# Attention units taken two at a time in the later batches of an attention and MLP kernel

## The chip, the cores and the metric

One core of one Trainium2 chip runs the whole program. The metric is the device time of one execution in microseconds (us), as the median of several runs. Its engines are TensorE (matrix products into the banks of PSUM), VectorE and ScalarE (elementwise work, and the only ones here that read PSUM), GpSimd (called POOL in the profile) and SyncE (SP, which issues most DMAs). Each works through its own instructions in order, and semaphores make one wait for another.

## What is computed

Three steps, in float32 at the interface: attention with two kinds of mask, a gated MLP, and an MLP with silu.

```python
# q, k, v: batch 4, 8 heads, 576 positions, head size 64; stride = 32
scores = scale * q @ k.T
mask_local   = (rel >= 0) & (rel < stride)                    # heads 0 to 3
mask_strided = (rel >= 0) & (pos_k % stride == pos_q % stride)  # heads 4 to 7
attn = softmax(where(mask, scores, -1e9))
x = (attn @ v), heads side by side: 2304 tokens x 512
y = ((x @ w_a) * (x @ w_b)) @ w_out          # inner size 1536
h = y @ w_in;  out = (h * sigmoid(h)) @ w_out2   # inner size 2048
```

## The kernel before

The tokens are cut into groups of 512 (the last has 256). Products are made in a split form: every operand is a pair of a rounded value and a remainder (`split_w`, `split_act`: ScalarE makes the first, VectorE the second), and each product takes three matmuls (`PASSES`). Batch 0's attention comes first, in a startup stage of its own. Then 136 **blocks** run, numbered p: for the first two groups the gated MLP (blocks 0 to 71), then the second MLP (72 to 135). A block is 12 matmuls of 128x128 by 128x512; its kind is a, b or o in the gated MLP (two up products and the down product) and i or p in the other. The loop over blocks stands at lines 1305 to 1379. After it come the other groups, in a form with fewer products.

Batches 1 to 3 of the attention are woven into the blocks 0 to 114. `PLAN` (line 96) gives for each batch a first block, the start of each of its nine **units**, and an end. Units 0 to 4 are the windows of 128 queries of the four local heads (unit 4 has 64); units 5 to 8 are groups of residues of the four strided heads (unit 8 has fewer). `plan_attention` (line 702) puts the steps of a unit with start s into blocks: `prepare` at s (for strided units VectorE gathers the queries), `scores`, `mask`, `largest`, `softmax`, `guard` and `normalise` at s+2, `turn` (transposing the weights on TensorE) and `turned` (copying them out of PSUM) at s+5, `values` (the products with v) and `store` at s+6. It also spreads the loads of later data, and the VectorE transposes of q and k (`transpose_qk`).

`block(p)` (line 739) sets the order in a block. At its head come the planned loads, TensorE steps and `turned` copies; then the block's 12 matmuls; then, in the order of the letters in `STEPS` (line 104), the rest: R prepare, M mask, 0 1 2 the steps that convert a weight (`merge_w`, one on ScalarE and two on VectorE), B a rescaling on ScalarE, K writing the converted weight to DRAM, O store, Y the split of the weight for block p+2, X softmax, W loads, N guard and normalise. In blocks 0 to 35 the order is RM0BK1O2YXWN, later 0O1B2MKWYRXN. The evacuation of the block's own product comes behind all of it: for a a copy on ScalarE; for b a product on VectorE, a cast on ScalarE and a subtraction on VectorE; for i a tanh on ScalarE and then the same three. Since every engine works in order, a step that waits holds up all that is behind it on that engine.

PSUM has eight banks: four accumulators, two in the ring for up products, and two for attention (`att_tile`, in turn, lines 187 to 196). In batches 1 to 3 a unit's scores take both attention banks, its turned weights one and its values one. `store` (line 542) copies the values on ScalarE; for the groups 0, 1 and 4 VectorE also takes the remainder out of the same bank.

The probabilities of softmax lie in three buffers by turns (`probs`, line 174), normalised by POOL at line 491.

Of the kernel before, what the change touches and what calls it, by code (L numbers as in the profile page):

```python
# [18 lines left out]
P = 128  # L19
STRIDE = 32  # L20
HALF = 64
TAKE = 3

RES = [(0, 3, 6), (9, 12, 15), (18, 21, 24), (27, 29)]
# [69 lines left out]


PLAN = {
# [3 lines left out]
}  # L100

PAIR_OF = (2, 3)

# [8 lines left out]
def attention_gated_mlp_silu_mlp(  # L112
# [15 lines left out]
    nc = tc.nc  # L128
# [7 lines left out]
    J = S // STRIDE  # L136
    NL = -(-S // P)
    JR = J * TAKE
    NG_S = max(map(len, RES))
    firsts = [r for i in RES for r in i]  # L140
    KV = HALF + JR
# [24 lines left out]
    ident = cpool.tile([P, P], F32, name="ident")  # L166
    ident_b = cpool.tile([P, P], BF16, name="ident_b")
# [4 lines left out]
    vs = apool.tile([P, len(firsts), 4, D], F32, name="vs", bufs=1)  # L172
# [60 lines left out]
    class Batch:  # L233
# [167 lines left out]
            st["parts"] = parts  # L401
            self.state[u] = st

        def scores(self, u):

            st = self.state[u]
            w, segs = st["w"], st["segs"]
            halves = [[part for part in st["parts"] if part[1] == hp] for hp in range(2)]
            if self.first:
                bank = att_tile(self.wide)[:, :segs * w].rearrange("p (s k) -> p s k", k=w)  # L410
                st["sc"] = [bank]
                for hp in range(2):
                    rows = slice(HALF * hp, HALF * (hp + 1))
                    nc.tensor.matmul(bank[rows], lhsT=ident_b[:, rows], rhs=st["mask"], start=True, stop=False)
                    for m, (_, _, s, rows, lhsT, rhs) in enumerate(halves[hp]):
                        last = m >= len(halves[hp]) - HALF // lhsT.shape[-1]
                        nc.tensor.matmul(bank[rows, s], lhsT=lhsT, rhs=rhs, start=False, stop=last)
                return
            per = segs // 2 if st["full"] else segs
            st["sc"] = [  # L420
                att_tile(self.wide)[:, :per * w].rearrange("p (s k) -> p s k", k=w) for _ in range(2)
            ]
            for half in range(2):
                for m in range(len(halves[0])):
                    for hp in range(2):
                        t, _, s, rows, lhsT, rhs = halves[hp][m]
                        bank = t if st["full"] else hp
                        if bank ^ hp == half:
                            nc.tensor.matmul(
                                st["sc"][bank][rows, s % per], lhsT=lhsT, rhs=rhs, start=True, stop=True  # L430
                            )

        def mask(self, u):
            st = self.state[u]
# [55 lines left out]
            rs = rs.unsqueeze(3).to_broadcast([P, ng, 2, w])  # L490
            nc.gpsimd.tensor_tensor(out=pr, in0=pr, in1=rs, op=ALU.mult)

        def turn(self, u):
            ty, i = self.units[u]
            st = self.state[u]
            nk = P if ty == 0 else KV
            pr = st["pr"].rearrange("p g s k -> p g (s k)")
            tp = att_tile(self.wide)
            for t in range(st["slots"]):
                nc.tensor.transpose(tp[:nk, P * t:P * (t + 1)], pr[:, t, :nk], ident)  # L500
            st["tp"] = tp

        def turned(self, u):
            ty, i = self.units[u]
# [12 lines left out]
                st["pt"] = pt = apool.tile([P, NG_S * P], F32, tag="pt", name="pt", bufs=2)  # L517
                copy(out=pt[:KV, :P * n], in_=st["tp"][:KV, :P * n])

        def values(self, u):  # L520
            ty, i = self.units[u]
            st = self.state[u]
            n, pt = st["n"], st["pt"]
            xp = st["xp"] = att_tile(self.wide)
            for hp in range(2):
                for g in range(st["slots"]):
                    for c in range(2):
                        h = 2 * hp + c
                        rows = xp[HALF * c:HALF * (c + 1), hp * n:(hp + 1) * n]
                        if ty == 0:  # L530
                            out = rows[:, HALF * g:HALF * (g + 1)]
                            lhsT = self.vl[:, 2 * i + g, h, :]
                            rhs = pt[:, g ^ hp if st["full"] else g, h, :]
                        else:
                            r0 = RES[i][g] - RES[i][0]
                            out = rows.rearrange("p (j r) -> p j r", j=J)[:, :, r0:r0 + TAKE]
                            lhsT = vs[:KV, firsts.index(RES[i][g]), h, :]
                            o = P * g + HALF * (hp if self.first else c)
                            rhs = pt[:KV, o:o + JR]
                        nc.tensor.matmul(out, lhsT=lhsT, rhs=rhs, start=True, stop=True)  # L540

        def store(self, u):
            ty, i = self.units[u]
# [33 lines left out]
    half = {"A": [], "B": []}  # L577
# [124 lines left out]
    def plan_attention(batch, s0, first, end):  # L702

        add = lambda at, place, f, *a: plan.setdefault((at, place), []).append((f, a))

        def spread(loads, n, s0, s1):
            for m in range(n):
                add(s0 + m * (s1 - s0) // n, "load", next, loads, None)

        turn1 = first[NL - 1] + 2  # L710
        for one in range(4):
            add(s0 + one // 2, "prepare", batch.transpose_qk, 0, one)
            add(turn1 - 4 + one, "prepare", batch.transpose_qk, 1, one)
        spread(batch.load_qk(1), 9, s0 + 2, turn1 - 7)
        spread(batch.load_vs(), 4 * TAKE + 5, s0 + 4 * (batch.b > 1), first[NL] + 3)
        for u, s in enumerate(first):
            add(s, "prepare", batch.prepare, u)
            add(s + 2, "tensor", batch.scores, u)
            add(s + 2, "mask", batch.mask, u)
            add(s + 2, "mask", batch.largest, u)  # L720
            add(s + 2, "softmax", batch.softmax, u)
            add(s + 2, "normalise", batch.guard, u)
            add(s + 2, "normalise", batch.normalise, u)
            add(s + 5, "tensor", batch.turn, u)
            add(s + 5, "turned", batch.turned, u)
            add(s + 6, "tensor", batch.values, u)
            add(s + 6, "store", batch.store, u)
        after = Batch(batch.b + 1, False)
        if after.b < B:
            spread(after.load_qk(0), 9, turn1 + 2, end)  # L730
            spread(after.load_vl(), 10, first[NL] + 7, end)
        return after

    def background(at, *places):
# [28 lines left out]
    with tc.manual_schedule():  # L763
# [51 lines left out]
        for s in range(-1, max(nu + LV, max(PART), max(CONV) + 1) + 1):  # L815
# [6 lines left out]
            now, last = CONV.get(s), CONV.get(s - 1)  # L822
            for step in ORDER:
# [13 lines left out]
                elif step == "A" and s in PART:  # L837
                    i = PART[s]
# [17 lines left out]
        batch = after  # L856
# [570 lines left out]
```

## Time and profile before

| | |
|---|---|
| median of 3 runs | 954.84 us (954.73 to 958.06) |
| span of the profiled execution, first to last instruction | 952.6 us |
| mean granted TensorE clock | 0.988 of full speed |
| TensorE matmul busy | 928.5 us, 97% |
| VectorE busy | 663.9 us, 70% |
| ScalarE busy | 542.6 us, 57% |
| POOL busy | 80.4 us, 8% |

The profile gives the span of its execution and no separate device time; the median lies 2.2 us above the span. Matmuls are pipelined and their ends are modelled, so TensorE's busy share says less than the starts of its runs and the waits between them. In the rows below, PE is TensorE's matmuls, DVE is VectorE, ACT is ScalarE; "out<-in" are the program's names of tiles, x12 is a count of records (a float32 matmul leaves two), and a bracket at the end is the time the engine sat idle before, with what ended it. A waits view names an engine and its line, what it waited for, the total, how many times and the longest.

### The profile page before, as it was taken

What the parts mean: (1) busy time and instruction counts of PE and PEld (TensorE: products, weight loads), DVE (VectorE), ACT (ScalarE), POOL (GpSimd) and SP (SyncE); (2) the same over time, 40 slices, a digit from 0 to 9 for tenths busy, and PEclk for the clock granted to TensorE, in tenths of its full rate; (3) what the DMA queues carried; (4) which work ended last, traced back from release to release, by engine and by line L of the source; (5) the groups of instructions that cost most, each with busy time, mean ns of one, the idle gap of its engine ahead of it and who ended that gap; (6) DMA issues with size and microseconds to landing.
All of it is one profiled execution on the core that took longest, in us unless ns stands there. A gap on an engine that the chain in (4) does not pass through costs nothing.

```text
span 952.6 us, 15861 instructions
## 1 busy us (share of the span) xinstructions
PE 928.5 (97%) x5626; PEld 749.6 (79%) x5626; DVE 663.9 (70%) x1248; ACT 542.6 (57%) x1274; POOL 80.4 (8%) x138
## 2 busy tenths in 40 slices
PE   9999999999999899999999999999999989999998
PEld 5767777787777677778888888888998768888897
DVE  4588888866767766666777666765587666765475
ACT  3558788566667665465544444345565555554364
POOL 2232222111111110100000000000000000000000
PEclk9799999999999999999999999999999999999999
DMA  9999899898698994322332222223464121234371
GB/s 165 198 271 269 248 254 271 248 294 240 224 267 208 264 223 133 105 86 89 100 105 83 67 67 67 57 83 112 126 185 125 44 67 56 78 107 148 108 212 47
DMA packets 163647, 145.29 MB, mean 153 GB/s; under 512 B 96800, under 2 KB 119904, under 8 KB 163568
## 3 DMA queue, kind: packets, MB, share of 16 engines
q1 hardware_dynamic: 154758, 121.81, 48.1%
q0 software_dynamic: 6720, 21.63, 6.8%
q10 hardware_dynamic: 2090, 0.84, 0.5%
q8 instruction: 44, 0.72, 0.3%
q14 instruction: 35, 0.29, 0.1%
HBM read 121.70 MB, written 22.54 MB: 151 GB/s over the span
## 4 chain that ended last, share of the span: by engine, by line
PE 75%; DVE 11%; ACT 8%; issue 3%; DMA 2%; SPq 0%; DVEq 0%; POOL 0%; ACTq 0%; POOLq 0%
PE ring L683 17%; PE ring L958 10%; PE att L958 8%; PE acc L1019 8%; PE acc L1365 7%; PE acc L1145 4%; PE att L1019 4%; PE ring L1019 4%; PE acc L1345 4%; PE acc L683 3%; ACT prs L466 2%; DVE w L676 2%; DVE raw L650 2%; PE att L540 1%; ACT raw L647 1%
## 5 line engine op out<-in xcount | busy, mean ns | idle before, releaser
L683 PE MATMUL ring<-x,w 128*128 128x512 f32 (+1 forms) x816 | 165.5, 356 | 1.5 <-DVE w L676 1.5
L683 PEld LDWEIGHTS ring<-x,w 128*128 128x128 f32 x816 | 132.4, 189 | 23.4 <-DVE w L676 2.0
L1241 DVE TENSOR_TENSOR w<-raw,w 128x512 fp32r<-128x512 f32 (+1 forms) x164 | 106.3, 656 | 30.3 <-ACT w L1240 27.5
L1240 ACT CAST w<-raw 128x512 fp32r<-128x512 f32 (+1 forms) x164 | 95.8, 593 | 18.6 <-PE att L1019 11.0
L676 DVE TENSOR_TENSOR w<-raw,w 128x512 fp32r<-128x512 f32 x136 | 92.8, 686 | 8.6 <-ACT w L675 7.9
L683 PE MATMUL ring<-y,w 128*128 128x512 f32 x384 | 96.1, 400 | 2.2 <-DVE g L1337 0.8
L1365 PE MATMUL acc<-w,h 128*128 128x512 f32 x384 | 93.9, 394 | 0.0
L683 PEld LDWEIGHTS ring<-y,w 128*128 128x128 f32 x384 | 71.9, 191 | 18.8 <-DVE w L676 1.1
L675 ACT CAST w<-raw 128x512 fp32r<-128x512 f32 x136 | 82.8, 619 | 4.0 <-DVE raw L655 3.9
L1365 PEld LDWEIGHTS acc<-w,h 128*128 128x128 f32 x384 | 70.9, 188 | 15.4
L693 ACT CAST h<-h 128x512 fp32r<-128x512 f32 (+1 forms) x48 | 27.3, 568 | 95.1 <-DVE h L1331 48.1
L1345 PE MATMUL acc<-h,w 128*128 128x512 f32 x288 | 70.8, 395 | 0.0
L958 PE MATMUL ring<-operands,w 128*128 128x512 f32 x240 | 61.4, 398 | 2.4 <-ACT w L1240 2.0
L694 DVE TENSOR_TENSOR h<-g,h 128x512 fp32r<-128x512 f32 (+1 forms) x64 | 39.9, 624 | 33.4 <-ACT h L693 33.2
L1345 PEld LDWEIGHTS acc<-h,w 128*128 128x128 f32 x288 | 53.0, 188 | 11.5
L693 ACT CAST h<-g 128x512 fp32r<-128x512 f32 (+1 forms) x64 | 36.3, 568 | 44.8 <-DVE g L1337 30.4
L958 PE MATMUL att<-operands,w 128*128 128x512 f32 x240 | 60.2, 395 | 0.0
L958 PE MATMUL ring<-x,w 128*128 128x512 f32 x240 | 59.2, 391 | 1.0 <-ACT u L969 1.0
L466 ACT ACTIVATE prs<-sm,nm 128x54 f32<-128x54 f32 (+1 forms) x120 | 39.8, 336 | 30.5 <-DVE nm L452 30.4
L958 PEld LDWEIGHTS ring<-operands,w 128*128 128x128 f32 x240 | 44.7, 188 | 14.8 <-ACT w L1240 2.7
L650 DVE SCALAR_TENSOR_TENSOR raw<-words,raw 128x512 int32<-128x512 int32 x68 | 47.6, 699 | 9.5 <-ACT raw L647 8.9
L958 PEld LDWEIGHTS ring<-x,w 128*128 128x128 f32 x240 | 44.9, 188 | 11.1 <-ACT u L969 1.4
(200 smaller groups left out, 1577.1 us busy)
## 6 DMA issues: line engine op xcount, KB each, us to landing
raw<-keptp SPq DMA_DIRECT2D x80, 256.0 KB
raw<-kepti SPq DMA_DIRECT2D x64, 256.0 KB
words<-in_moe_w_out_dram SPq DMA_DIRECT2D x28, 512.0 KB
raw<-kepto SPq DMA_DIRECT2D x48, 256.0 KB
raw<-kepta SPq DMA_DIRECT2D x36, 256.0 KB
raw<-keptb SPq DMA_DIRECT2D x36, 256.0 KB
words<-in_moe_w_in_dram SPq DMA_DIRECT2D x16, 512.0 KB
words<-in_moe_w_a_dram SPq DMA_DIRECT2D x12, 512.0 KB
```

What stands on the lines that cost most here:

```text
L466: nc.scalar.activation(out=place[s], in_=src[:, s], func=AF.Exp, bias=st["nm"][:, s:s + 1], scale=1.0, accum_out=su[:, s:s + 1],)
L650: nc.vector.scalar_tensor_tensor(out=z, in0=high, scalar=SIGN, in1=z, op0=ALU.bitwise_and, op1=ALU.bitwise_or)
L675: nc.scalar.copy(out=o[:, 0], in_=t)
L676: nc.vector.tensor_tensor(out=o[:, 1], in0=t, in1=o[:, 0].bitcast(F32), op=ALU.subtract)
L683: nc.tensor.matmul(ps[:, :T], lhsT=w[:, wi, c * P:(c + 1) * P], rhs=x[:, xi, c, :T], start=(c == 0 and wi == 0 and xi == 0), stop=(c == CC ...
L693: nc.scalar.copy(out=o[:, 0, :T], in_=t32[:, :T])
L958: nc.tensor.matmul(self.acc[acc], lhsT=w[:, wi, (2 * part + c) * P:(2 * part + c + 1) * P], rhs=x[:, xi, c], start=(begin and c == 0 and m ...
L1019: nc.tensor.matmul(accs[d], lhsT=lhsT, rhs=rhs, start=(first and wi == 0 and xi == 0), stop=(last and wi == 1))
L1240: nc.scalar.copy(out=o[:, 0, cols], in_=t)
L1241: nc.vector.tensor_tensor(out=o[:, 1, cols], in0=t, in1=o[:, 0, cols].bitcast(F32), op=ALU.subtract)
L1345: nc.tensor.matmul(accs[d], lhsT=w[:, wi, d * P:(d + 1) * P], rhs=h[:, xi], start=(j == 0 and wi == 0 and xi == 0), stop=(j == N1 - 1 and ...
L1365: nc.tensor.matmul(accs[t][:, :DM], lhsT=h[:, xi, t * P:(t + 1) * P], rhs=w[:, wi, :], start=(j == 0 and wi == 0 and xi == 0), stop=(j == ...
```

## The change

Units are taken in the groups of `TOGETHER`: (0, 1), (2, 3), (4), (5, 6), (7, 8). `PLAN` holds a start for each group. The scores of both units of a group are issued in one run of TensorE, each unit in its own 256 columns of the same two banks; so are both turns, and both units' products with v. Two local units share one bank for the turned weights and one for the values; two strided units take a bank each. With a group's start s, prepare is at s-1 and s, scores at s+2, the masks and softmaxes of the two units at s+2 and s+3, both turns and copies at s+6, both values and stores at s+7 (a single unit as before). In batches 2 and 3 the four transposes of q and k at the batch's start go one to a block instead of two, and the loads of the other heads begin two blocks later. Batch 0 computes as before.

```diff
 PLAN = {
-    1: (0, [1, 2, 7, 8, 13, 18, 19, 24, 25], 35),
-    2: (35, [38, 43, 48, 53, 58, 63, 68, 73, 78], 80),
-    3: (81, [84, 85, 90, 91, 96, 101, 102, 107, 108], 0),
+    1: (0, [2, 8, 14, 19, 25], 35),
+    2: (35, [39, 48, 57, 64, 73], 80),
+    3: (81, [84, 90, 96, 101, 107], 0),
 }
+TOGETHER = ((0, 1), (2, 3), (4,), (5, 6), (7, 8))
...
+        def scores_together(self, us):
+            banks = [att_tile(self.wide) for _ in range(2)]
+            for n, u in enumerate(us):
+                st = self.state[u]
+                w = st["w"]
+                st["per"] = per = st["segs"] // 2 if st["full"] else st["segs"]
+                o = 256 * n
+                st["sc"] = [b[:, o:o + per * w].rearrange("p (s k) -> p s k", k=w) for b in banks]
             for half in range(2):
-                for m in range(len(halves[0])):
+                for u in us:
...
+        def shared(self, us):
+            bank = None
+            for n, u in enumerate(us):
+                if n == 0 or self.units[u][0] == 1:
+                    bank, o = att_tile(self.wide), 0
+                yield u, bank, o
+                o += 256
+
+        def turn(self, *us):
+            for u, bank, o in self.shared(us):
...
+                st["tp"] = tp = bank[:, o:]
...
+        def values(self, *us):
+            for u, bank, off in self.shared(us):
...
+                xp = st["xp"] = bank[:, off:]
...
         for one in range(4):
-            add(s0 + one // 2, "prepare", batch.transpose_qk, 0, one)
+            add(s0 + (one if batch.b > 1 else one // 2), "prepare", batch.transpose_qk, 0, one)
             add(turn1 - 4 + one, "prepare", batch.transpose_qk, 1, one)
-        spread(batch.load_qk(1), 9, s0 + 2, turn1 - 7)
+        spread(batch.load_qk(1), 9, s0 + (4 if batch.b > 1 else 2), turn1 - 7)
...
+        for us, s in zip(TOGETHER, first):
+            others = len(us) - 1
+            add(s + 2, "tensor", batch.scores, *us)
+            for n, u in enumerate(us):
+                add(s + n - others, "prepare", batch.prepare, u)
+                add(s + n + 2, "mask", batch.mask, u)
+                add(s + n + 2, "mask", batch.largest, u)
+                add(s + n + 2, "softmax", batch.softmax, u)
+                add(s + n + 2, "normalise", batch.guard, u)
+                add(s + n + 2, "normalise", batch.normalise, u)
+                add(s + others + 5, "turned", batch.turned, u)
+                add(s + others + 6, "store", batch.store, u)
+            add(s + others + 5, "tensor", batch.turn, *us)
+            add(s + others + 6, "tensor", batch.values, *us)
```

## Rows read from the trace of the kernel before

**Rows 1.** The page, shares of the span on the chain that ended last, by engine

```profile
PE 75%; DVE 11%; ACT 8%; issue 3%; DMA 2%; SPq 0%; DVEq 0%; POOL 0%; ACTq 0%; POOLq 0%
```

**Rows 2.** Busy us by stage: PE, PEld, DVE, ACT, POOL; then clock, DMA share, GB/s

```profile
67.99:175.34 107.35, 105.13 (x739) 82.36 (x734) 89.78 (x180) 84.18 (x215) 22.74 (x40) 1.00 0.98 265
...
180.22:288.27 108.05, 107.64 (x719) 85.50 (x719) 76.39 (x142) 67.66 (x170) 14.55 (x25) 1.00 0.90 256
288.27:339.89 51.62, 46.76 (x281) 35.99 (x279) 38.22 (x72) 34.05 (x84) 6.98 (x12) 0.97 0.94 240
339.89:439.89 100.00, 97.35 (x762) 75.99 (x761) 64.31 (x140) 58.94 (x175) 10.76 (x16) 1.00 0.46 126
...
439.89:952.60 512.71, 503.87 (x2485) 423.51 (x2483) 346.40 (x606) 259.77 (x492) 6.51 (x12) 1.00 0.32 97
```

**Rows 3.** TensorE timeline in batch 2: start, us, line, out<-in, count

```profile
197.08 0.38 PE L500 MATMUL att<-ident,prs 128*128 128x128 f32 x2
197.21 3.02 PE L1345 MATMUL acc<-h,w 128*128 128x512 f32 x12
200.16 0.69 PE L540 MATMUL att<-ptl,vl 128*64 128x64 f32 x16
200.78 3.01 PE L683 MATMUL ring<-x,w 128*128 128x512 f32 x12
203.72 0.70 PE L429 MATMUL att<-kT,qT 64*32 64x64 f32 x32
204.35 3.01 PE L683 MATMUL ring<-x,w 128*128 128x512 f32 x12
207.20 2.88 PE L1345 MATMUL acc<-h,w 128*128 128x512 f32 x12
209.92 2.89 PE L683 MATMUL ring<-x,w 128*128 128x512 f32 x12
```

**Rows 4.** TensorE's waits from 63 to 440 us: total, times, longest

```profile
PE att L540 <- ACT pt L518: 3.3, 2, 2.8
PE att L540 <- ACT ptl L512: 2.4, 3, 1.3
PE ring L683 <- DVE w L676: 2.3, 2, 1.5
...
PE ring L683 <- DVE g L1337: 0.8, 1, 0.8
```

**Rows 5.** VectorE timeline, the middle of block 25

```profile
143.53 0.42 DVE L571 TENSOR_TENSOR x<-att,x 128x252 fp32r<-128x252 f32 x1
143.87 0.68 DVE L655 SCALAR_TENSOR_TENSOR raw<-e,raw 128x512 int32<-128x512 int32 x1
144.47 0.69 DVE L676 TENSOR_TENSOR w<-raw,w 128x512 fp32r<-128x512 f32 x1
```

**Rows 6.** VectorE timeline, the transposes in blocks 35 and 81

```profile
176.76 1.43 DVE L275 STREAM_TRANSPOSE qT<-qld 128x576 f32<-128x576 f32 x2
...
325.69 1.43 DVE L275 STREAM_TRANSPOSE qT<-qld 128x576 f32<-128x576 f32 x2
```

**Rows 7.** ScalarE timeline, the copy ahead of unit 8's values in batch 2

```profile
331.57 0.37 ACT L518 COPY pt<-att 118x256 f32<-118x256 f32 x1
```

**Rows 8.** Busy times of block 84's products, columns as in rows 2

```profile
332.60:337.04 4.44, 4.44 (x16) 3.50 (x13) 2.48 (x4) 1.80 (x5) 0.54 (x1) 0.62 0.95 245
```

**Rows 9.** TensorE timeline, the attention runs at blocks 73 and 74

```profile
290.99 0.49 PE L500 MATMUL att<-ident,prs 128*118 128x128 f32 x3
...
296.17 0.91 PE L540 MATMUL att<-pt,vs 118*64 118x54 f32 x24
```

**Rows 10.** VectorE timeline, first conversion step and softmax guard of block 75

```profile
303.71 0.69 DVE L650 SCALAR_TENSOR_TENSOR raw<-words,raw 128x512 int32<-128x512 int32 x1
...
308.37 0.17 DVE L478 TENSOR_SCALAR su<-su 128x6 f32<-128x6 f32 x1 [1.58 <-ACT prs L466]
```

**Rows 11.** ScalarE timeline, the second of block 25's two store copies

```profile
143.29 0.21 ACT L568 COPY x<-att 128x72 f32<-128x72 f32 x1
```

More of the change, by code (lines that the diff above doesn't have):

```diff
@@ L402, in prepare, with scores @@
             self.state[u] = st
-        def scores(self, u):
+        def scores(self, u, *more):
+            if not self.first:
+                return self.scores_together((u, *more))
             st = self.state[u]
@@ L408, in scores @@
             halves = [[part for part in st["parts"] if part[1] == hp] for hp in range(2)]
[L409 to L422, printed above, removed]
-            for half in range(2):
-                for m in range(len(halves[0])):
[L425 to L431, printed above, removed]
+            bank = att_tile(self.wide)[:, :segs * w].rearrange("p (s k) -> p s k", k=w)
@@ new lines, in scores @@
+            st["sc"] = [bank]
+            for hp in range(2):
+                rows = slice(HALF * hp, HALF * (hp + 1))
+                nc.tensor.matmul(bank[rows], lhsT=ident_b[:, rows], rhs=st["mask"], start=True, stop=False)
+                for m, (_, _, s, rows, lhsT, rhs) in enumerate(halves[hp]):
+                    last = m >= len(halves[hp]) - HALF // lhsT.shape[-1]
+                    nc.tensor.matmul(bank[rows, s], lhsT=lhsT, rhs=rhs, start=False, stop=last)
+        def scores_together(self, us):
[6 more added lines that the diff above has]
+                st["sc"] = [b[:, o:o + per * w].rearrange("p (s k) -> p s k", k=w) for b in banks]
+            for half in range(2):
+                for u in us:
+                    st = self.state[u]
+                    halves = [[part for part in st["parts"] if part[1] == hp] for hp in range(2)]
+                    for m in range(len(halves[0])):
+                        for hp in range(2):
+                            t, _, s, rows, lhsT, rhs = halves[hp][m]
+                            bank = t if st["full"] else hp
+                            if bank ^ hp == half:
+                                nc.tensor.matmul(
+                                    st["sc"][bank][rows, s % st["per"]], lhsT=lhsT, rhs=rhs, start=True, stop=True
+                                )
@@ L491, in normalise @@
             nc.gpsimd.tensor_tensor(out=pr, in0=pr, in1=rs, op=ALU.mult)
[L493 to L501, printed above, removed]
+        def shared(self, us):
[7 more added lines that the diff above has]
+            for u, bank, o in self.shared(us):
+                ty, i = self.units[u]
+                st = self.state[u]
+                nk = P if ty == 0 else KV
+                pr = st["pr"].rearrange("p g s k -> p g (s k)")
+                st["tp"] = tp = bank[:, o:]
+                for t in range(st["slots"]):
+                    nc.tensor.transpose(tp[:nk, P * t:P * (t + 1)], pr[:, t, :nk], ident)
         def turned(self, u):
@@ L518, in turned @@
                 copy(out=pt[:KV, :P * n], in_=st["tp"][:KV, :P * n])
[L520 to L540, printed above, removed]
@@ new lines, in values @@
+        def values(self, *us):
+            for u, bank, off in self.shared(us):
+                ty, i = self.units[u]
+                st = self.state[u]
+                n, pt = st["n"], st["pt"]
+                xp = st["xp"] = bank[:, off:]
+                for hp in range(2):
+                    for g in range(st["slots"]):
+                        for c in range(2):
+                            h = 2 * hp + c
+                            rows = xp[HALF * c:HALF * (c + 1), hp * n:(hp + 1) * n]
+                            if ty == 0:
+                                out = rows[:, HALF * g:HALF * (g + 1)]
+                                lhsT = self.vl[:, 2 * i + g, h, :]
+                                rhs = pt[:, g ^ hp if st["full"] else g, h, :]
+                            else:
+                                r0 = RES[i][g] - RES[i][0]
+                                out = rows.rearrange("p (j r) -> p j r", j=J)[:, :, r0:r0 + TAKE]
+                                lhsT = vs[:KV, firsts.index(RES[i][g]), h, :]
+                                o = P * g + HALF * (hp if self.first else c)
+                                rhs = pt[:KV, o:o + JR]
+                            nc.tensor.matmul(out, lhsT=lhsT, rhs=rhs, start=True, stop=True)
@@ L708, in spread @@
                 add(s0 + m * (s1 - s0) // n, "load", next, loads, None)
-        turn1 = first[NL - 1] + 2
+        starts = {us[0]: s for us, s in zip(TOGETHER, first)}
+        first1 = starts[NL]
+        turn1 = starts[NL - 1] + 2
         for one in range(4):
-            add(s0 + one // 2, "prepare", batch.transpose_qk, 0, one)
+            add(s0 + (one if batch.b > 1 else one // 2), "prepare", batch.transpose_qk, 0, one)
             add(turn1 - 4 + one, "prepare", batch.transpose_qk, 1, one)
-        spread(batch.load_qk(1), 9, s0 + 2, turn1 - 7)
[L715 to L727, printed above, removed]
+        spread(batch.load_qk(1), 9, s0 + (4 if batch.b > 1 else 2), turn1 - 7)
+        spread(batch.load_vs(), 4 * TAKE + 5, s0 + 4 * (batch.b > 1), first1 + 3)
+        for us, s in zip(TOGETHER, first):
[12 more added lines that the diff above has]
+            add(s + others + 6, "tensor", batch.values, *us)
         after = Batch(batch.b + 1, False)
@@ L730, in plan_attention @@
             spread(after.load_qk(0), 9, turn1 + 2, end)
-            spread(after.load_vl(), 10, first[NL] + 7, end)
+            spread(after.load_vl(), 10, first1 + 7, end)
         return after
```

## The prediction

> **What bounds the kernel now.** I read four views, in this order. The page's shares of the chain of waits come first [rows 1]: three quarters of the span lie on TensorE, a fifth on VectorE and ScalarE together. So time taken off TensorE counts, but not everywhere. The busy times by stage say where [rows 2]. By the TensorE timeline the first four rows are blocks 4 to 35, blocks 37 to 71, 72 to 85, and 86 to 114; the last is all that follows. In the first, VectorE is busy 89.8 of 107.35 us, ScalarE 84.2 and TensorE 105.1: three engines near their limit. In the second and fourth TensorE alone is near it (107.64 of 108.05, 97.35 of 100.00). In the third TensorE is idle 4.9 us of 51.62. Behind block 114, where the changed code ends, TensorE is busy 503.9 of 512.7 us, so what is won until then should stay to the end.
>
> Third, the TensorE timeline at small scale [rows 3]. A plain block of 12 products takes 207.20 to 209.92, 2.72 us. Between a turn and a run of values a block lasts 197.21 to 200.16, 2.95; between values and scores 2.94; between scores and a plain block 2.85. So leaving attention costs about 0.13 and entering scores or values about 0.10 (leaving values some 0.03 more; entering a turn nothing, 0.23 being one exit and one entry). I call that the switch: 0.23 for a run of scores, 0.13 for a turn, 0.26 for values. The runs themselves (0.13, 0.62 and 0.63 for one unit of the local heads) stay as they are: the same matmuls are issued.
>
> Fourth, what TensorE waits for between 63 and 440 us [rows 4]: ScalarE's copies of the turned weights ahead of the values (3.3 and 2.4 us), the split weights (2.3), and a bank held by VectorE's gate (0.8). These waits can weigh as much as all the switches, so they decide.
>
> **The change part by part.** *Fewer runs.* In batches 1 and 3 the units of a pair already start one block apart. A pair there has two score runs, a turn, a joint run (values of the first, turn of the second) and a values run. The joint run's switch is not in my rows; it lies between 0.26 and 0.39, the sum of its two kinds, and I take 0.30: 0.46 + 0.13 + 0.30 + 0.26 = 1.15. After, three runs: 0.23 + 0.13 + 0.26 = 0.62. Four pairs save 2.1 us in each of these batches. In batch 2 the units stand five blocks apart, six runs for two units, 1.24; four pairs save 2.5. Together 6.7 us of TensorE time, if nobody else is late.
>
> *Blocks 4 to 36 (batch 1).* Here VectorE decides. The last place where TensorE waits for it is the scores of unit 7 at block 26, which need unit 6's subtraction out of the bank; that begins at 143.53 and ends at 143.95 [rows 5]. After the change both subtractions of the pair are issued in block 26 and the joint scores in block 27. VectorE then has ahead of them what was behind: the two last steps of block 25 and the first of block 26, three of 0.60 by the spacing of the rows, so 145.8. From unit 7's scores to block 36 TensorE took 143.95 to 175.34, 31.4 us; block 26's products (2.7) now lie ahead, and this pair's switches shrink by 0.5: 28.2, hence 174.0. A gain of 1.3. Its ends: nothing, if ScalarE's copies for two units in one block delay VectorE further, and 3.4, if the two engines run ahead a block earlier (2.1 from the switches and the 1.3).
>
> *The transposes of the next batch.* Batch 2's q and k are transposed on VectorE, two in block 35 (1.4 us from 176.76 [rows 6]) and two in block 36, ahead of the split for block 37, on which TensorE waits up to 1.5 us. One per block takes 0.7 off that wait; nothing if VectorE has other work in the hole. I take 0.7. The later ones lie in blocks where TensorE has two blocks of lead.
>
> *Blocks 37 to 85 (batch 2).* Switches give 2.5. Block 84 held the longest wait, 2.8 us: TensorE wants unit 8's values, but VectorE did transposes from 325.69 on [rows 6] ahead of a gate, ScalarE had to cast that gate's result, and the copy of the turned weights began only at 331.57 [rows 7]. Behind it the granted clock averaged 0.62 in the 4.44 us of block 84's products [rows 8], that is, TensorE fell to its lower level of 1.2 GHz after that idle; 1.6 us lost against 2.85. Unit 8 now ends at block 80, before those transposes, so both go: 4.4. Block 73 took from 290.99 to 296.17, 5.2 us with a turn of 0.24 in it [rows 9], 2.0 more than 2.95, since unit 6's softmax sat ahead of the evacuation of y. The softmax moves to block 67; instead two units' stores (some 0.7 of ScalarE) come into block 71. Walking the copies through I leave 0.7 of the wait: 1.3 won. One of the three waits on the local copies [rows 4], 0.4 at block 59, goes.
>
> Added: units 7 and 8 have masks and softmaxes in blocks 75 and 76, one behind the other. Block 75's VectorE steps take 303.71 to 308.54 [rows 10], 4.8 us in 6 instructions, 1.58 of it waiting for ScalarE's softmax in its own queue. A second such block behind it makes 9.6, against 7.0 for TensorE (two blocks and two units' scores). Queued behind the waiting VectorE are the split weights for blocks 77 to 79. Of TensorE's lead of two blocks most is used up by then, as block 73's wait shows; with 2.6 more and the conversions of block 77 behind it I estimate 3.5 of waits in blocks 77 to 80. The ends are zero (the lead holds) and 5.1 (the clock falls again as well, 1.6). Net 2.5 + 4.4 + 1.3 + 0.4 - 3.5 = 5.1.
>
> *Blocks 86 to 114 (batch 3).* Switches 2.1. The first values waited 1.3, the longest of the waits on the local copies [rows 4]; now the turn falls behind a block without a cast, but four copies come together instead of two: 0.45 left, 0.85 won. The wait for the gate at block 106 (0.8) is set by VectorE; with a turn (0.24) and two switches (0.36) taken from ahead of it TensorE comes 0.6 earlier and waits that much longer. The first strided pair's values wait some 0.25 more than the 0.5 they do now (3.3 less 2.8). Net 2.1 + 0.85 - 0.6 - 0.25 = 2.1, between 0 and 3.5.
>
> At no cost: the loads moved by a block or two on SP's queue (no row of TensorE's waits names a DMA), the slices of the shared banks (256 columns hold the widest unit's 162), and POOL's normalising, which keeps at least three blocks before its turn.
>
> *Sum:* 1.3 + 0.7 + 5.1 + 2.1 = 9.2 us. The profiled span of 952.6 becomes 943.4; the median, 954.84, stands 2.2 above that span, so the forecast is 945.6.
>
> **The rivals.** *A shared bank is read by one engine at a time.* In block 25 ScalarE's second copy out of the bank, which is not an operand of the subtraction, ended at 143.50 [rows 11], and VectorE's subtraction from that bank began at 143.53 [rows 5]. If so, in blocks 9 and 15 (local pairs sharing a bank, with both copy and subtraction) the second unit's copy waits for the first's subtraction, 0.42 and a restart, about 0.6 each time: 1.2 less won, 946.8. The Trainium skill, "PSUM — Partial Sum Buffer", section "PSUM bank collisions raise a hardware error", says that two engines may not touch one bank in the same quadrant at a time, reads included, so that the order must be enforced; by that rule the sharing has this price, and the trace agrees as far as one row can.
>
> *VectorE and ScalarE hand it all back.* They never wait long for TensorE in stages one and three, and their work is the same. Then the 6.7 us of switches turn into new waits: 9.2 - 6.7 = 2.5 won, 952.3. For it speaks the first stage, against it the second, where TensorE has no waits to speak of.
>
> *Longer waits ahead of the values: slower.* A pair's values need both units' copies, put into one block. In six places (blocks 25, 31, 70, 79, 107, 113) that block follows one whose gate result ScalarE must cast first, as in block 83. If ScalarE is a block late there, each is a wait like block 84's, with the clock behind it: 2.8 + 1.6 = 4.4. Two undo the gain; from the third on the kernel is slower: 945.6 + 13.2 = 958.8. Against it: two strided units' copies cost 0.37 + 0.47, about one local unit's pair (0.75), and of the five such waits so far four were 1.3 or less.
>
> *The lead holds.* No new wait in blocks 77 to 80 (3.5), and batch 1 wins 3.4: 14.5 won, 940.3.
>
> **How the numbers follow.** Forecast 945.6 with 0.44; the one-engine bank 946.8 with 0.20; the lead holds 940.3 with 0.10; handed back 952.3 with 0.18; slower 958.8 with 0.08. The measurement can tell about 0.5%, 4.8 us, from no change: below 950.1 is faster, which the first three are (0.74); the fourth is the same (0.18); the last slower (0.08). The range, 939.5 to 952.5, takes in the bounds of the unknown waits and leaves out the slower case and a rest of the others.
>
> **What would show it.** Right: block 36 begins 1 to 2 us earlier, block 84 has no wait and the clock there is 1.00, block 86 begins some 7 us earlier, block 115 some 9; the block behind a turn of two units still takes 2.95. Wrong: waits over 2 us on ScalarE's copies of the turned weights at blocks 26, 71, 80 or 108; a clock of 0.5 near block 79; scores waiting over 1 us for the stores at blocks 10, 16 and 27; or a joint run of two units longer than two single ones, which would mean that sharing a bank costs TensorE itself.

## The result: 948.44 us, and where the 0.85% came from

The changed kernel has a median of 948.44 us in its runs (945.97 to 951.47); the kernel before, beside it, 954.84 (952.84 to 958.21). One more execution of the changed kernel, at a mean granted clock of 0.85, took 1006.47; it is counted in the median, but in neither the range nor the ratio. The ratio of time after to time before is 0.9915, 95% interval 0.9887 to 0.9942: about 8.1 us won (5.5 to 10.8), 6.4 by the medians, where 9.2 were forecast. The profiled execution has a span of 946.7 us against 952.6.

In the changed kernel the lines have moved: 440 scores, 454 mask, 477 softmax, 521 turn, 532 and 538 the copies of the turned weights, 561 values, 589 and 592 the store's copy and subtraction, 697 split weights, 1362 gate, 1088 results. Two lines of the page of after, the busy time of TensorE and the shares on the chain that ended last (75% of it on TensorE before, [rows 1]):

```profile
PE 918.6 (97%) x5620; PEld 746.9 (79%) x5626; DVE 663.4 (70%) x1248; ACT 541.8 (57%) x1274; POOL 80.2 (8%) x138
...
PE 69%; DVE 13%; ACT 8%; issue 5%; DMA 3%; SPq 1%; POOL 0%; DVEq 0%; ACTq 0%; POOLq 0%
```

TensorE is busy 9.9 us less than before, and the chain leans more on VectorE. Next the busy times in three stretches, first of the kernel before, then of after. The cuts are the same events in both: the split of weights by VectorE just ahead of batch 1's first scores (59.40 and 57.47), TensorE's restart in block 37, the scores at block 86, and the end of batch 3's last values.

```profile
59.40:180.22 120.82, 114.85 (x825) 89.29 (x823) 102.00 (x202) 93.78 (x238) 23.11 (x41) 0.99 0.94 256
180.22:339.89 159.67, 154.40 (x998) 121.49 (x998) 114.61 (x214) 101.71 (x252) 21.53 (x37) 0.99 0.91 251
339.89:437.09 97.20, 94.55 (x750) 73.71 (x749) 63.32 (x138) 58.05 (x172) 10.76 (x16) 1.00 0.47 126
```

```profile
57.47:179.06 121.59, 112.02 (x824) 88.11 (x822) 102.50 (x201) 93.47 (x238) 23.78 (x41) 1.00 0.96 262
179.06:333.49 154.43, 150.87 (x999) 120.19 (x999) 113.59 (x213) 100.68 (x250) 21.01 (x37) 1.00 0.91 254
333.49:431.14 97.65, 94.15 (x750) 75.04 (x749) 63.26 (x137) 58.97 (x174) 10.72 (x16) 0.98 0.50 134
```

Read the first number behind each stretch. Batch 1 takes 0.8 us longer than before, batch 2 with what follows it 5.2 less, batch 3 0.45 longer. At block 115 the changed kernel is 5.96 us ahead (433.93 against 439.89), and it stays so to the end (512.77 us behind that point, 512.71 before). But 5.2 less 0.8 and 0.45 is 4.0. The other 1.93 us stand there at the first cut already, ahead of all the scores that the change joins: 59.40 against 57.47. Most of it, 1.69, is there at an earlier split, inside batch 0, which computes as before; VectorE in before, then in after:

```profile
46.59 0.69 DVE L676 TENSOR_TENSOR w<-raw,w 128x512 fp32r<-128x512 f32 x1
```

```profile
44.90 0.66 DVE L697 TENSOR_TENSOR w<-raw,w 128x512 fp32r<-128x512 f32 x1
```

In the ten kernels whose traces are told of here this step begins between 43.1 and 47.1 us, three kernels with the old order among them at 43.1, 46.4 and 46.6. The clock went with it. From the start to the first cut, before and then after (the last figures of a row are the mean granted clock, the share of the DMA engines and GB/s):

```profile
0.00:59.40 59.40, 58.06 (x562) 39.32 (x563) 36.61 (x91) 28.45 (x119) 18.53 (x33) 0.89 1.00 201
```

```profile
0.00:57.47 57.47, 54.88 (x556) 37.78 (x562) 36.40 (x91) 28.35 (x119) 18.24 (x33) 0.94 0.97 193
```

In the ten traces the first cut lies at 56.4 us with a clock of 0.97 up to it, at 57.5 to 57.8 with 0.94 (three), at 59.2 to 60.5 with 0.88 or 0.89 (three, one of them in the new order and two in the old), and at 59.6 and 59.8 with 0.86; the tenth, at 61.9 with 0.99, waited 6.1 us for a load. So the 1.93 us go with the clock of these two executions and not with the order of the units. Stages are compared below from cut to cut, and totals by the ratios alone.

What TensorE waited for in after, from 60 to 440 us (total, times, longest; before: [rows 4]):

```profile
PE att L561 <- ACT ptl L532: 3.2, 5, 1.0
PE att L440 <- DVE x L592: 2.8, 2, 1.6
PE ring L704 <- DVE g L1362: 2.1, 1, 2.1
PE ring L704 <- DVE w L697: 1.8, 2, 1.3
PE att L561 <- ACT pt L538: 1.7, 3, 1.2
PE acc L1390 <- ACT w L696: 1.2, 1, 1.2
```

The wait of 2.8 at block 84 is gone. Three others have grown: scores that wait for the subtractions of the store (2.8 in two places, blocks 10 and 16; 1.1 before), the gate at block 106 (0.8 before, 2.1 now), and, in batch 1, values that wait for ScalarE's copies of the turned weights (0.7 before, 3.6 now; the rows stand with the account of blocks 4 to 36).

Joint runs do what they should. Batch 2, units 2 and 3, TensorE's timeline of after:

```profile
230.02 0.60 PE L521 MATMUL att<-ident,prs 128*128 128x128 f32 x4
230.37 2.99 PE L704 MATMUL ring<-x,w 128*128 128x512 f32 x12
233.29 1.15 PE L561 MATMUL att<-ptl,vl 128*64 128x64 f32 x32
234.37 2.79 PE L1370 MATMUL acc<-h,w 128*128 128x512 f32 x11
```

Two units' values take 233.29 to 234.37, 1.08 us, where two runs of one took 0.62 each [rows 3]; the block behind the two-unit turn (0.35 us) lasts 2.92.

### The profile page after: what moved, and what is told of

Its sections match the earlier page's. It is cut to its first block, busy times and chain, and to the rows that moved or that the text cites. A ratio compares the mean times of both kernels' runs of the same rounds, so it can differ in the third digit from the quotient of the medians.

```text
span 946.7 us, 15843 instructions
## 1 busy us (share of the span) xinstructions
PE 918.6 (97%) x5620; PEld 746.9 (79%) x5626; DVE 663.4 (70%) x1248; ACT 541.8 (57%) x1274; POOL 80.2 (8%) x138
## 4 chain that ended last, share of the span: by engine, by line
PE 69%; DVE 13%; ACT 8%; issue 5%; DMA 3%; SPq 1%; POOL 0%; DVEq 0%; ACTq 0%; POOLq 0%
PE ring L704 14%; PE ring L983 11%; PE att L983 8%; PE acc L1044 8%; PE acc L1390 6%; PE acc L1170 4%; PE att L1044 4%; PE ring L1044 4%; ACT prs L477 3%; PE acc L1370 3%; PE acc L704 2%; DVE w L697 2%; DVE raw L671 2%; DMA kepti<-raw 1%; DVE raw L676 1%
## 5 line engine op out<-in xcount | busy, mean ns | idle before, releaser
L983 PEld LDWEIGHTS ring<-operands,w 128*128 128x128 f32 x240 | 44.7, 188 | 14.8 <-ACT w L1265 2.7
L671 DVE SCALAR_TENSOR_TENSOR raw<-words,raw 128x512 int32<-128x512 int32 x68 | 47.6, 700 | 10.8 <-ACT raw L668 10.2
```

What stands on the lines that cost most here:

```text
L671: nc.vector.scalar_tensor_tensor(out=z, in0=high, scalar=SIGN, in1=z, op0=ALU.bitwise_and, op1=ALU.bitwise_or)
L983: nc.tensor.matmul(self.acc[acc], lhsT=w[:, wi, (2 * part + c) * P:(2 * part + c + 1) * P], rhs=x[:, xi, c], start=(begin and c == 0 and m ...
```

## Experiments

All ratios are to the kernel before; those of one group of runs share its runs.

**Units one at a time, at the new places.** This takes the joint runs away and keeps the plan, except that the first unit of a pair has its turn and values one block earlier than in the changed kernel.

```diff
-    1: (0, [2, 8, 14, 19, 25], 35),
+    1: (0, [2, 3, 8, 9, 14, 19, 20, 25, 26], 35),
...
-TOGETHER = ((0, 1), (2, 3), (4,), (5, 6), (7, 8))
+TOGETHER = tuple((u,) for u in range(9))
```

(Batches 2 and 3 likewise.)

> The units stand in the changed kernel's blocks (the second of a pair one block behind the first), but each unit's scores, turn and values are TensorE runs of their own. If the joint runs bring the gain (switches of 0.23, 0.13 and 0.26 us): four pairs in each of three batches pay 0.53 us more, 6.4 us in all, so 0.998 of before. If the new places bring it (block 84 without its wait, block 73 shorter): 0.992, like the changed kernel. Block 84 has no wait by both.

Measured: 951.75 us, ratio 0.9950 (0.9930 to 0.9969). So of about 8 us the places alone bring 4.8 (3.0 to 6.7). That leaves 3.3 for the joint runs, uncertain by about 3 (an estimate from the two intervals); the two traces are 1.2 apart from the first cut to the last values (374.89 and 373.67). By stage the split is uneven:

```profile
59.21:179.13 119.92, 112.73 (x822) 87.31 (x820) 102.30 (x201) 92.92 (x237) 23.80 (x41) 1.00 0.92 262
179.13:336.13 157.00, 153.77 (x998) 121.54 (x998) 114.02 (x213) 101.15 (x251) 21.02 (x37) 0.99 0.91 250
336.13:434.10 97.97, 94.33 (x749) 73.56 (x748) 63.84 (x138) 58.91 (x174) 10.73 (x16) 1.00 0.51 134
```

In batch 1 single units are quicker than joint ones (119.92 against 121.59, and 121.1 to 121.2 in two further kernels with joint ones below): joining costs there. With a bank for each unit's values (the next run, and the last) joint units take 120.0 and 120.5, so most of that cost is the shared bank's. In batch 2 single units are 2.6 slower (157.00 against 154.43). Block 84 has no wait, but another place has one, since unit 8's scores at block 76 need banks that unit 7's scores fill until its mask has read them:

```profile
303.81 0.87 PE L440 MATMUL att<-kT,qs 64*64 64x54 f32 x16 [2.44 <-DVE sm L454]
304.61 4.61 PE L704 MATMUL ring<-y,w 128*128 128x512 f32 x12
```

and the twelve products behind that wait of 2.44 took 4.61 us instead of 2.9. These 4.1 us at one place are more than the whole difference in batch 2, so it isn't the switches alone that the joint runs save there.

**Values of a local pair in banks of their own.** The only edit is that each unit's values get a bank; scores and turns stay joined.

```diff
         def values(self, *us):
-            for u, bank, off in self.shared(us):
+            for u, bank, off in ((u, att_tile(self.wide), 0) for u in us):
```

> The changed kernel, but two local units' values lie in a bank each. If one engine at a time may read a bank: ScalarE's second store copy in blocks 9 and 15 no longer waits for VectorE (0.49 and 0.84 us in the changed kernel), the scores at blocks 10 and 16 wait some 0.5 us less each, and block 36 begins up to 1 us earlier: 0.9905 of before. If VectorE's own chain sets batch 1's pace: those waits shift, block 36 begins within 0.3 us of the changed kernel, 0.9915.

Measured: 946.29 us, ratio 0.9899 (0.9865 to 0.9933). From the first cut to block 37 it takes 120.00 us against 121.59, and the two waits of scores for the subtractions fall from 1.20 and 1.60 to 0.60 and 0.94. What they were is seen on ScalarE and VectorE in block 9 of the changed kernel:

```profile
84.33 0.35 ACT L589 CAST x<-att 128x256 fp32r<-128x256 f32 x1
85.17 0.37 ACT L589 CAST x<-att 128x256 fp32r<-128x256 f32 x1 [0.49 <-DVE x L592]
```

```profile
84.71 0.42 DVE L592 TENSOR_TENSOR x<-att,x 128x256 fp32r<-128x256 f32 x1
85.57 0.42 DVE L592 TENSOR_TENSOR x<-att,x 128x256 fp32r<-128x256 f32 x1 [0.44 <-ACT x L589]
```

The second unit's copy waits for the first unit's subtraction, though it doesn't use what that writes, and the second subtraction waits for its copy: one engine at a time on a bank, in a chain of four. With own banks the two subtractions run as one row, 0.76 us:

```profile
86.80 0.76 DVE L592 TENSOR_TENSOR x<-att,x 128x256 fp32r<-128x256 f32 x2
```

**Two transposes per block again,** with the loads left where the change put them.

```diff
-            add(s0 + (one if batch.b > 1 else one // 2), "prepare", batch.transpose_qk, 0, one)
+            add(s0 + one // 2, "prepare", batch.transpose_qk, 0, one)
```

> The changed kernel, but two transposes of q and k per block at a batch's start, as before. By the sum of the prediction the wait at block 37 grows by 0.7 us and nothing else does: 0.9922 of before. If the split for block 37 waits for something else (block 37 gained only some 0.2 us): within 0.2 us, 0.9917. If the old wait at block 84 came from the transposes alone, not from the values standing there: a wait of over 1 us comes back near blocks 83 to 85.

Measured: 947.9 us, ratio 0.9913 (0.9882 to 0.9945); the time can't tell it from the changed kernel. The wait at block 37 can: 1.34 us in after, 2.01 here.

```profile
179.06 8.00 PE L704 MATMUL ring<-x,w 128*128 128x512 f32 x34 [1.34 <-DVE w L697]
```

```profile
181.91 9.59 PE L704 MATMUL ring<-x,w 128*128 128x512 f32 x34 [2.01 <-DVE w L697]
```

So spreading the transposes is worth 0.67 us of that wait between these two traces. In the four traces with two transposes in a block the wait is 1.55 to 2.33, in the six with one 0.88 to 1.35. Behind the longer wait the same 34 records took 9.59 us instead of 8.00, at a granted clock of 0.82 of full speed on the mean: 1.6 us more in this execution.

**Half of the first group's results on ScalarE.** At block 106 TensorE waits for VectorE's gate. Ahead of that gate VectorE copies four results (2.44 us); here ScalarE takes two of them.

```diff
-                result(t0, t, accs[t], pool, tag, "v", nc.gpsimd)
+                result(t0, t, accs[t], pool, tag, "va"[t % 2] if g == 0 else "v", nc.gpsimd)
```

> The changed kernel, but of the four evacuations of results behind block 103 ScalarE takes two, VectorE two. If VectorE's four in a row make the gate late for which block 106 waits (2.1 us, with the clock at 0.62 behind it): the wait falls to about 0.9, the clock stays at 1.00, 2.8 us less: 0.9885 of before. If the wait comes from the softmax that VectorE waits for in its queue (1.58 us): the wait stays above 1.8 and the time within 0.5 us of the changed kernel, 0.991.

Measured: 946.78 us, ratio 0.9895 (0.9866 to 0.9925). The wait goes from 2.13 to 0.93, by just what the copies shrank (2.44 to 1.25), and block 106's products are at full clock. The step in the ratio, from 0.9915, lies within the intervals. First after, then this kernel:

```profile
401.17 4.61 PE L704 MATMUL ring<-y,w 128*128 128x512 f32 x12 [2.13 <-DVE g L1362]
```

```profile
400.49 3.04 PE L704 MATMUL ring<-y,w 128*128 128x512 f32 x12 [0.93 <-DVE g L1362]
```

**The same edit in the kernel before,** as a control.

> The kernel before with half of the first group's results copied by ScalarE instead of VectorE. There the wait for the gate at block 106 was 0.78 us with the full clock behind it. If the results matter only because the two-unit runs made VectorE late there, this gains at most those 0.78 us: ratio 0.998 to 1.000, and block 106 without a wait. If the results are a cost in themselves, the gain is that of the changed kernel with the same edit beside it (some 1.2 us and a low clock of 1.6): ratio 0.997 or less.

Measured: ratio 1.0006 (0.9979 to 1.0034). The wait of 0.78 at block 106 is gone in its trace, and nothing can be told in the time. What hung on the results before the change was at most that wait; the trace of the changed kernel has 1.2 us of wait and the low clock on them.

**The joint scores at block 103 undone,** for batch 3's first strided pair alone.

```diff
+            if batch.b == 3 and us == (5, 6):
+                add(s + 2, "tensor", batch.scores, 5)
+                add(s + 3, "tensor", batch.scores, 6)
+            else:
                 add(s + 2, "tensor", batch.scores, *us)
```

> The changed kernel, with the scores of batch 3's first strided pair in two runs again, at blocks 103 and 104; its masks, turn and values stay where they are. In the changed kernel the first mask of this pair began 1.50 us after the first score, in the kernel before 0.87 us. If the joint scores make VectorE late at block 106 by these 0.63 us, the wait for the gate there falls from 2.13 to about 1.3 (0.63, and one more switch of 0.23 ahead of it), block 115 begins 0.4 us earlier, and by 1.6 more where the low clock behind the wait goes too. If the wait comes only from TensorE being earlier, it falls by the 0.23 alone, to 1.9. The total is too close to the changed kernel's to be told apart by time: ratio 0.988 to 0.992 either way.

Measured: 947.83 us, ratio 0.9898 (0.9874 to 0.9921). The wait is 1.10. First after: the start of the scores on TensorE, then mask and gate on VectorE. Then the same rows with the scores apart.

```profile
389.19 1.44 PE L440 MATMUL att<-kT,qs 64*64 64x54 f32 x48
...
390.69 0.56 DVE L454 SCALAR_TENSOR_TENSOR sm<-att,mask_str 128x162 f32<-128x162 f32 x2 [2.55 <-PE att L440]
...
400.42 0.69 DVE L1362 SCALAR_TENSOR_TENSOR g<-th,ring 128x512 f32<-128x512 f32 x1
```

```profile
389.11 0.82 PE L440 MATMUL att<-kT,qs 64*64 64x54 f32 x24
...
389.98 0.56 DVE L454 SCALAR_TENSOR_TENSOR sm<-att,mask_str 128x162 f32<-128x162 f32 x2 [1.93 <-PE att L440]
...
399.71 0.69 DVE L1366 SCALAR_TENSOR_TENSOR g<-th,ring 128x512 f32<-128x512 f32 x1
```

The first mask starts 1.50 us behind the first score when the scores are joined, 0.87 when not, since the half that fills the second bank is issued behind both units' first halves. The gate begins a full chain later (mask, softmax, results, second mask, second softmax), and the 0.63 go through it undiminished: 11.23 us from score to gate against 10.60. The other 0.40 of the 1.03 by which the wait fell are TensorE's own: from its first score to the start of the wait it takes 10.25 us with the scores apart and 9.85 with them joined. A joint run makes the first unit wait for the second.

**Places alone, in the kernel before.** Only batch 2's starts are moved, so that unit 8's values stand at block 80.

```diff
-    2: (35, [38, 43, 48, 53, 58, 63, 68, 73, 78], 80),
+    2: (35, [38, 43, 48, 53, 57, 61, 66, 70, 74], 80),
```

> The kernel before with units one at a time, and only batch 2's starts moved: its last five units start 1 to 4 blocks earlier, so that unit 8's values stand at block 80 instead of 84, as in the changed kernel. If the place alone was block 84's loss (its wait of 2.8 us and the 1.6 us of low clock behind it), block 84 has no wait, the scores at block 86 begin some 4.4 us earlier than at 339.89, and the ratio is 0.995 to 0.996. If the loss hangs on VectorE being behind in batch 2 whatever stands at block 84, a wait of over 2 us turns up elsewhere between blocks 70 and 85, and the ratio stays within 0.002 of 1. If the two-unit runs were needed for the gain, block 84 still waits.

Measured: 953.5 us, ratio 0.9966 (0.9946 to 0.9986). Block 84 has no wait, so it was the place. But of the 4.4 us at stake the ratio shows 3.3 with an interval from 1.3 to 5.2, and in the trace the stretch from block 37 to block 86 is no shorter at all (159.86 us against 159.67). A fall of the clock at block 37, which is not this edit's, takes 1.6 of it; the rest goes to new waits and to a second fall behind two of them: units four blocks apart put the scores of one unit right behind the values of another, and they wait for ScalarE's copies out of the bank. Its waits from 181 to 341 us:

```profile
PE att L429 <- ACT x L568: 3.2, 4, 1.5
PE ring L683 <- DVE w L676: 1.9, 1, 1.9
PE att L540 <- ACT pt L518: 0.9, 1, 0.9
PE att L540 <- ACT ptl L512: 0.4, 1, 0.4
```

One block apart, as in the first experiment, single units wait for banks at block 76 instead. The five groups have neither neighbourhood: in batch 2, between one group's values and the next one's scores lie at least three blocks.

**Both mends together:** own banks for the values, and half of the results on ScalarE.

> The changed kernel with both mends: the values of a local pair in banks of their own, and half of the first group's results on ScalarE. If the two losses add up, the waits for the stores at blocks 10 and 16 fall by 1.3 us together, that for the gate at block 106 by 1.2, and the low clock of 1.6 behind it goes: block 115 begins some 4 us earlier than in the changed kernel (433.93) and the ratio to the kernel before is about 0.987. If a wait that is won in batch 1 is lost again at block 37, where VectorE's split weights come late, the first 1.3 us are gone and the ratio is 0.989.

Measured: 944.4 us, ratio 0.9862 (0.9833 to 0.9891), the best of all kernels run here. Its stages:

```profile
56.38:176.84 120.46, 111.97 (x825) 88.09 (x823) 102.26 (x201) 93.27 (x238) 23.80 (x41) 1.00 0.95 266
176.84:330.93 154.09, 150.79 (x998) 120.20 (x998) 113.57 (x213) 100.73 (x250) 20.99 (x37) 1.00 0.92 253
330.93:425.82 94.89, 92.53 (x750) 73.81 (x749) 61.52 (x135) 59.50 (x176) 10.70 (x16) 1.00 0.53 141
```

Batch 1 takes 1.1 us less than in the changed kernel, batch 3 2.8 less. The waits for the stores sum to 1.5 (2.8), the gate's is 0.94, and the clock is at 2.4 GHz through all three. The two losses add up as the first of the two expectations had it: some 4 us between the first cut and block 115.

## Why the prediction came out, and which of its terms did not

The total was right and the sign was; the working was right in batch 2 and wrong in batches 1 and 3. That 9.2 lies so near to 8.1 is in good part luck: the stages of the two traces make up 4.0 of it, and the terms that came out (batch 2, the transposes) are 5.8 of the 9.2. By steps:

**Blocks 4 to 36: forecast +1.3, found nothing.** Block 36 does begin 0.95 earlier (174.39), but the execution was already 1.93 ahead at the first cut. The step that failed is the start of block 27's scores, forecast at 145.8 with VectorE as the one engine that decides. From them to block 36 TensorE took 28.3 us, as forecast (28.2). But it came to them at 146.06, which is 147.99 with the 1.93 added, and without a wait there: VectorE's subtractions had ended at 145.85, just ahead. So both engines were some 2 us behind the forecast. On the way TensorE had waited longer. Its waits for the stores and for ScalarE's copies ahead of the values, from the first cut to block 37, before and then after (that for the stores is 2.8 after):

```profile
PE att L429 <- DVE x L571: 1.1, 2, 0.9
PE att L540 <- ACT ptl L512: 0.7, 1, 0.7
```

```profile
PE att L561 <- ACT ptl L532: 2.1, 3, 0.9
PE att L561 <- ACT pt L538: 1.5, 2, 1.2
```

The waits for the copies were an end of this term's range and had no place in its middle. Also, an earlier block 36 wouldn't have been enough: at block 37 TensorE waits for VectorE's split in both kernels, and, counted from the first cut, this split came later than before. From the first cut to block 37 the changed kernel needs 121.59 us, 120.82 before; with half the results on ScalarE and with the scores apart (batch 1 as in the changed kernel) the stretches are 121.2 and 121.1, in the two other kernels with the old batch 1 they are 121.1 and 121.7. So nothing is won there that can be told from the spread, the lower of the two ends given. VectorE is busy 102 us of it in all cases, and TensorE's gain became waits. That was the rival "VectorE and ScalarE hand it back", and it held in this stage only. The price of the one-engine bank was right: forecast 1.2, measured 1.3 in the two waits, and in the stage 0.6 to 1.6 (120.0 and 120.5 in the two kernels with own banks against 121.1 to 121.6 in three without). The waits for the copies stay with own banks (3.7); what they cost by themselves no run separates. The rival was thus true, but as a part beside the forecast and not instead of it. The Trainium skill, "PSUM — Partial Sum Buffer", section "PSUM bank collisions raise a hardware error", states that two engines may not touch the same quadrant of a bank at once, reads by ScalarE and VectorE included. The trace agrees with the order that this asks for: the waits of 0.49 and 0.44 in block 9 are what keeping it costs.

**Transposes: forecast +0.7, worth 0.67,** as undoing them shows. In the comparison of before and after it hardly shows (1.55 to 1.34): counted from the first cut, block 36 begins 0.98 later and the split for block 37 comes 0.77 later, so VectorE had lost more in batch 1 than the transposes gave back.

**Blocks 37 to 85: forecast +5.1, found 5.2.** The terms: block 84's wait and its low clock 4.4, both gone; block 73 and its neighbours 1.2 (2.1 of waits before, 0.37 and 0.51 after), forecast 1.3; new waits in blocks 77 to 79 0.19 + 0.49 + 1.17 + 0.34 = 2.2, forecast 3.5 for blocks 77 to 80; switches 1.9 (TensorE's busy time fell by 3.5, of which 1.6 is the clock), forecast 2.5. For the local pairs the 0.62 each is right: from the first scores to unit 4's, before took 62.75 us for 20 blocks, after 55.77 for 18; less 2.72 per block and the waits of 0.41 and 0.18 that leaves 7.94 and 6.63, 1.31 for two pairs. The strided pairs must then have given the smaller part. Block 59's wait of 0.41 is gone, but one of 0.18 has come at block 46: 0.2, forecast 0.4. By these readings the terms sum to 5.5, against 5.24 between the cuts; the new waits were put too high by 1.3, the switches by 0.6, and the errors nearly cancel.

**Blocks 86 to 114: forecast +2.1, found -0.45.** The failed term is the gate's wait at block 106. It was put at 0.8 plus 0.6 for TensorE's earlier arrival, and it is 2.13. Missing are the 0.63 by which a joint run of scores delays the first mask, and so the whole chain up to the gate; the scores apart show them. Behind this wait the clock fell, which the forecast had allowed for only at block 79: block 106's products go from 401.17 to 405.61, at a mean granted clock of 0.62, a part of them at 1.2 GHz, and cost 1.5 us more. The window in after, columns as in [rows 2]:

```profile
401.17:405.61 4.44, 4.44 (x12) 3.44 (x13) 3.13 (x6) 2.75 (x5) 0.14 (x1) 0.62 0.22 59
```

The first values' wait was forecast at 0.45 and is 0.98, still less than 1.3; the strided values, forecast 0.25 worse, are 0.36 better. The switches were right: TensorE's busy time fell by 0.4 with 1.5 more of low clock in it, so by 1.9, forecast 2.1. The argument against the slower rival, that two strided units' copies cost about as much as one local unit's pair, held: no wait on turned copies is over 1.2 us. The lesser waits of this kind are those of batch 1 above.

**Of the signs to look for,** "block 84 without a wait" and the block behind a turn (2.92) were met; "block 36 1 to 2 us earlier" and "block 86 some 7 us earlier" were not: 0.95 and 6.4 in the traces are a loss of 0.98 and a gain of 4.5 when the 1.93 of the start are taken off; "scores waiting over 1 us for the stores" came at blocks 10 and 16, named as a sign that the forecast is wrong, and it was there; block 115 is 6.0 earlier (4.0 from the first cut) instead of 9. Two sums are a little off: each execution's time lies 1.8 above its own span, not 2.2, and the rival "the lead holds" adds up to 14.8 and not 14.5; neither changes a choice.

**What stays open.** The two traces, cut to cut, show 4.0 us, the ratio 8.1 (5.5 to 10.8). Part of the gap is that a trace is one execution: that of before has a span of 952.6 where 19 executions of this kernel have 954.2 in the mean (949.1 to 958.3); that of after has 946.7 where six have 946.4. The trace of before also has no fall of the clock behind its wait at block 37, and the two other kernels with the old order have one, of about 1.6 us. Spans go with the mean granted clock: at 0.987 to 0.989 eleven executions of before average 954.8 and two of after 949.0; at 0.995 and 0.996 four average 952.0 and three 945.3. So by an estimate from these some 6 us are won at equal clock, and the rest goes with a higher mean clock after (0.9935 against 0.9895 and 0.9908 in two groups of runs). Part of the mean clock is that of the start, which the change leaves alone. How much is the change's own, and whether what the trace of before shows at single places is typical, one trace for each kernel can't tell.

## What to carry to other kernels

Joining two units' TensorE runs saves the switches only where TensorE is the late engine; where VectorE has the longer queue the same edit makes the first unit's mask, and all behind it, wait for the second unit. Look at which engine each stage waits for before counting saved TensorE time, and follow the first unit's chain to the next product that needs VectorE. Put operands that two engines read in turn into banks of their own when there are banks to spare, and move a unit away from the block where VectorE has its one-off work: the second was worth more here (4.4 us at block 84 by the traces) than the switches of any one batch (1.9), the first about 1.

## What the runs showed of the hardware

**The clock behind a wait.** TensorE fell to its lower level behind some waits and not behind others of nearly the same length. The wait at block 106 was 2.13, 2.13 and 2.12 us in three kernels (changed, own banks, two transposes): the twelve records behind it took 4.61, 4.61 and 3.06 us. Here the middle of those and the last:

```profile
400.94 4.61 PE L704 MATMUL ring<-y,w 128*128 128x512 f32 x12 [2.13 <-DVE g L1362]
```

```profile
404.90 3.06 PE L704 MATMUL ring<-y,w 128*128 128x512 f32 x12 [2.12 <-DVE g L1362]
```

At block 37 the waits of 0.88 to 1.55 us in seven kernels were followed by 8.0 us for 34 records; those of 1.86, 2.01 and 2.33 in three by 9.6. But in the kernel with places alone the clock also fell behind two waits of 0.87 and 0.83 close together. Each fall cost about 1.5 us. The mean granted clock of one and the same program's executions differs too (0.988 to 0.998 in six of the changed kernel), so a single trace holds one of several outcomes; at which places other executions fall, no run here shows.
